# A gated attention kernel in fp32 on one core: the first norm shared out anew, the last products in halves, statistics transposed by VectorE, a sigmoid at the seventh step, a new order of up products and splits

## The chip, the core and the metric

One core of a Trainium2 chip runs the whole kernel. TensorE multiplies, VectorE, ScalarE and GpSimd (POOL) prepare operands and evacuate results, and SyncE (SP) issues most of the DMAs. The metric is the device time of one execution in microseconds; three executions of the kernel before were timed. A profile is one more execution, recorded instruction by instruction.

## The reference

The inputs are `x` (2048 tokens of 640), a key and value cache of 32 heads of which the last 512 positions are used (`W = max(256, 2048 // 4)`), and four weight matrices. Cut to what is computed:

```python
xn = layernorm(x)                                   # over 640, no gain
q = (xn @ wq) split into 32 heads of 128
p = softmax(q k^T * 128 ** -0.5)                    # k, v: the last 512 cached positions
s = (p @ v, heads joined: 4096) @ wo
h = relu(xn @ w1 + b1) ** 2                         # 640 -> 1728
g = silu(h @ w2 + b2)                               # 1728 -> 640
out = x + s * g
```

All of it is float32. The kernel multiplies in TensorE's fp32r form and splits each operand in a high part (a ScalarE copy into fp32r) and a low part (the difference, on VectorE or POOL). A product is then three matmuls, high by high, high by low and low by high (`triple`).

## The kernel before

Tokens are worked in four tiles of 512 (`t` = 0 to 3), columns of `x` in five chunks of 128 (`DC`), the hidden width 1728 in fourteen chunks (`FC`), of which one, `rp` (placed fourth), has 64 columns. The order of the instructions on each engine is the order in which the program text emits them (`Ordered`, line 65); the attention part builds a list of (time, function) pairs, `plan`, and emits it sorted by time.

1. **The first norm** (`ln_first`). Tile 0's four blocks of 128 tokens (`xn[0]` to `xn[3]`) are loaded. VectorE takes mean and variance of each (`bn`, `aggr` into `mv`); blocks 0 and 1 are the first half, 2 and 3 the second. `root(k)` takes the square root of a half's variances on ScalarE and adds eps on VectorE. A reciprocal and a Newton step follow, on POOL for the first half and on VectorE for the second. ScalarE centres and scales blocks 0 and 1 (`centre`, `scale`); VectorE subtracts and multiplies blocks 2 and 3 in one instruction per block and column range (first 256 columns, then 384). TensorE transposes each block chunk by chunk (`turn`) into the five banks `px`; ScalarE copies them out as the high part of `xT` and VectorE takes the low part. The first up product `ph` (`up(0, 0)`, 15 matmuls in an order written out by hand) follows, with the transpose of the bias rows `pb` and what hangs on it (`biases`) behind its sixth matmul.
2. **Tile 0's feed-forward** with the norms of tiles 1 and 2 beside it (`first_step`): per step `f`, an up product of 15 matmuls and the down product of the chunk before, 15 more into the five banks `py`. Weights come in by SP two chunks ahead. The statistics of a later tile lie one token to a partition in `mv` (mean and 1/sd of four blocks: 8 columns). `ln_rows` turns them to rows: a TensorE transpose `pmv`, a copy `lr`, one DMA to DRAM, then two broadcasting loads `mr`. `ln_chunk` uses them two steps later. Tile 3 (`LATE`) gets the same at the last weight pair.
3. **Tiles 1 and 2's up products** in pairs of weight chunks, seven products for eight (`PROD`, `w_first` to `w_third`). VectorE forms sums of the weights (`w_sums`, tile `ws`), ScalarE and VectorE split them (`w_split`, tiles `wa`, `ws`, `wc`, `wl`). The first bank `wa` holds products 1, 6, 7 and 4 in turn; `wy` takes product 5, is copied to `p`, and becomes `wa + p` on VectorE; `wx` likewise after product 7. Between these lie tile 0's gates (`gate`, a sigmoid on ScalarE and a product on VectorE, tile `sg`).
4. **The down products of tiles 1 and 2**, 28 steps `m` of 15 (`c_down`), with operands loaded three steps and split two steps ahead (`c_load`, `c_prep`). After step 13 stands the gate of tile 1, whose five banks the products of tile 2 reuse.
5. **Attention**, 128 units of one head by one tile, a new one each `PERIOD` of 12.4 in the plan. A unit's work: scores `s`, the row maxima by a transposing reduction `rdm`, the shift and exponential `e`, `pt` split on ScalarE and POOL, `o`, and the output product `r`; q products `pq` for two units ahead alternate with these. Into units 0 to 3 goes also the rest of tile 3's up products for the last four chunks (`early_up`, banks `eu`, order in `EARLY_IN`). q products and some of `r` share bank 1.
6. **The end.** Tile 3's feed-forward follows the last unit (`lu`, `ly`). The last four down chunks (`FA` to `FC - 1`) are done column by column (kind `e`, line 1493): 12 matmuls for column `d`, then `late_gate(d)`, a silu, a product with the attention sum `acc`, an addition of `x` and a store. The last column's gate is done in two halves of 256 tokens.

`pe.addr_align` (lines 272, 1317, 1376) puts some TensorE instructions at fixed places of a 256-instruction block.

Of the kernel before, what the change touches and what calls it, by code (L numbers as in the profile page):

```python
# [25 lines left out]
def kernel(  # L26
# [115 lines left out]
    def ln_load(t):  # L142
        mv = xp.tile([P, 4, NB], F32, tag="mv", name=f"mv{t}")[:, :2, :]
        sc = xp.tile([P, 3, NB], F32, tag="sc", name=f"sc{t}")
        xn = []
        for b in range(NB):
            xb = ln_tile(t, b)
            r0 = t * NT + b * P
            nc.sync.dma_start(xb, x[r0 : r0 + P, :])
            xn.append(xb)  # L150
        LS[t] = mv, sc, xn

    def ln_block(t, b):
# [5 lines left out]
        dve.bn_aggr(mv[:, :, b], st)  # L159

# [16 lines left out]
    def ln_rows(t, mv):  # L177
        pm = psx.tile([P, NT], F32, tag="x", name=f"pmv{t}")
        (pe if t == LATE else nc.tensor).transpose(pm[: 2 * NB, :P], mv.rearrange("p a b -> p (a b)"), ident)
        row = xp.tile([2 * NB, P], F32, tag="lr", name=f"lr{t}", bufs=1)  # L180
        nc.vector.tensor_copy(row, pm[: 2 * NB, :P])
        d = dpool.tile([2, NT], F32, name=f"mv_d{t}")
        nc.sync.dma_start(d.rearrange("a (b p) -> (a b) p", p=P), row)
# [65 lines left out]
    def ln_first():  # L249
        mv = xp.tile([P, 4, NB], F32, tag="mv", name="mv0")  # L250
        sc = xp.tile([P, 3, NB], F32, tag="sc", name="sc0")
# [3 lines left out]
        VAR, SD, Y = ([sc[:, i, n * k : n * k + n] for k in range(2)] for i in range(3))  # L255
        warm = mv[:, 3, :1]
        pool.memset(warm, 1.0)
        eps = mv[:, 3, 1:2]
# [45 lines left out]
        def scale(b, cs):  # L304
            js = slice(cs[0] * P, (cs[-1] + 1) * P)
            act.activation(xn[b][:, js], xn[b][:, js], AF.Identity, scale=R[0][:, b : b + 1])

# [14 lines left out]
        centre(1)  # L322
        bn(n, 0)
        dve.reciprocal(Y[0], SD[0])
        newton(0)
        bn(n, 1)
        aggr(n)
        for b in range(n + 1, NB):
            for i in range(2):
                bn(b, i)  # L330
            aggr(b)
        scale(0, range(3))
        root(1)
        scale(0, range(3, DC))
        turn(0, range(DC))
        scale(1, range(DC))
        split_hi(0, raws[0], 0)
        dve.reciprocal(Y[1], SD[1])
        newton(1)
        for cs in (range(2), range(2, DC)):  # L340
            js = slice(cs[0] * P, (cs[-1] + 1) * P)
            for b in range(n, NB):
                m, q = mv[:, 0, b : b + 1], mv[:, 1, b : b + 1]
                dve.tensor_scalar(
                    xn[b][:, js], xn[b][:, js], m, q, op0=ALU.subtract, op1=ALU.mult
                )
            for c in cs:
                for b in range(1, NB):
                    turn(b, (c,))
# [108 lines left out]
    def up(t, f):  # L458
# [15 lines left out]
        for k, (c, i, j) in enumerate(order):  # L474
            pe.matmul(
                ph,
                w[i][:, c, :],
                xs[j][:, c, :],
                start=k == 0,
                stop=k == len(order) - 1,  # L480
            )
            if t == f == 0 and k == 5:
                biases()
# [200 lines left out]

    def w_second(p):
        b = PB[p]
        prod(p, 6, b["a"])
        dve.tensor_tensor(b["y"], b["a"], b["p5"], op=ALU.add)
        prod(p, 2, b["x"])
        rest(p, 0, 0, b["x"])  # L690
        up_end(T1, PAIRS[p][0], b["x"])
# [487 lines left out]
    def late_down(f, ds):  # L1179
# [6 lines left out]
        for d in ds:  # L1186
            dd = slice(d * P, (d + 1) * P)
            if n < P:
                pe.matmul(LPY[d], w[0][:, dd], h[0], start=False, stop=False)
                pe.matmul(LPY[d], w[1][:, dd], h[0], start=False, stop=False)  # L1190
            else:
                triple(
                    LPY[d], (w[0][:, dd], w[1][:, dd]), tuple(h), f == 0, f == FC - 1
                )

# [4 lines left out]

    def late_gate(d):
        py, a = LPY[d], ACC[HALF - 1, TPH - 1][:, d, :]
        sg = ap.tile([P, NT], F32, tag=("bm", "bs")[d % 2], name=f"lsg{d}", bufs=2)
        k = 2 if d == DC - 1 else 1
        js = [slice(i * NT // k, (i + 1) * NT // k) for i in range(k)]
        for j in js:
            act.activation(sg[:, j], py[:, j], AF.Silu, bias=b2_sb[:, d : d + 1])
        for j in js:
            dve.tensor_tensor(a[:, j], sg[:, j], a[:, j], op=ALU.mult)
            dve.tensor_tensor(a[:, j], a[:, j], LR["x"][:, d, j], op=ALU.add)  # L1210
            store(sp, HALF - 1, TPH - 1, d, a, j)

# [16 lines left out]
    w_sums(1)  # L1229
    w_split(1, 0)  # L1230
    w_fifth(0)
    w_second(0)
    gate(0, gate_tile, (3, 4))
    w_split(1, 1)
    w_split(1, 2)
    NP = len(PAIRS)
    for p in range(1, NP):
# [5 lines left out]

        def prepare():
            if more:
                w_split(p + 1, 0)
                w_sums(p + 1)
            else:
                for k in range(2):
                    c_prep(0, k)  # L1250
# [22 lines left out]
    xctx.close()  # L1273
    bctx.close()
    for m in range(2 * FC):
        t, f = CS[m]
        for n in {OPEN + 2: (m + 3, m + 4), OPEN + 3: ()}.get(m, (m + 3,)):
            if n < 2 * FC:
                c_load(n)
# [110 lines left out]
    for i in range(NU):  # L1390
# [65 lines left out]
    for item in order:  # L1456
# [9 lines left out]
        else:  # L1466
            for k, d in enumerate(range(DC)):
                for f in range(FA, FC):
                    DOWN_AT.setdefault(f, now)
                    at(now + 0.68 * ((FC - FA) * k + f - FA), late_down, f, (d,))  # L1470
                at(now + 0.68 * (FC - FA) * (k + 1), late_gate, d)
        now += STEP[kind]
# [110 lines left out]
```

## Time and profile before

| | us |
|---|---|
| median of three runs | 1951.23 (1951.10 to 1951.89) |
| the profiled execution | 1951.11 |
| its span, first to last instruction of the program | 1949.3 |
| TensorE busy | 1941.4, 8576 matmuls |
| VectorE, ScalarE, POOL busy | 1599.3, 1242.6, 1346.5 |
| TensorE's clock as granted | 1.0 |
| HBM traffic | 246.43 MB moved, mean 126 GB/s |

How to read it: a page row of a group has the engine, the operation, what it writes and reads, the shape, the count, busy time, the mean of one in nanoseconds, and the idle time before it with what ended it. A row of the timeline has its start, its length, the engine, the operation and the count of merged instructions, with the idle time before in brackets. A row of the chain of waits has a start, a length and the work that the end hung on then. PEld is the loading of weights, which overlaps the matmuls. A name with q (SPq) is the engine's queue issuing a DMA. Nearly every instruction is recorded in one helper (line 77), so groups are told apart by their tiles.

### The profile page before, as it was taken

Reading aid. Unit: us, or ns where it says so; the run is one execution under the profiler, and the core shown is the slowest. Engines: PE = TensorE matmul, PEld = TensorE weight load, DVE = VectorE, ACT = ScalarE, POOL = GpSimd, SP = SyncE. Lnnn points to the kernel's source line nnn. Section 1 sums busy time; section 2 is a strip of 40 time slices with the busy share of each in tenths; the row PEclk is TensorE's granted clock in tenths of the full one; section 3 lists DMA queues with packets and bytes.
Section 4 is the critical chain, followed back from the end, with each engine's and each line's share of the span. In section 5 each row is a group of like instructions: output and inputs, shape, how many; then the busy total and the mean of one; then the engine's idle time right before and its main releaser. Section 6 shows DMA issues by size and latency. Waiting matters only on the chain.

```text
span 1949.3 us, 28584 instructions
## 1 busy us (share of the span) xinstructions
PE 1941.4 (100%) x8576; PEld 1605.5 (82%) x8576; DVE 1599.3 (82%) x2758; ACT 1242.6 (64%) x2150; POOL 1346.5 (69%) x727
## 2 busy tenths in 40 slices
PE   9999999999999999999999999999999999999998
PEld 7888888888888888888888888888888888888887
DVE  6864747788888888888888878888888888888864
ACT  5665536766666666666666676666666666666643
POOL 0022107888888888888888878888888888888841
PEclk9999999999999999999999999999999999999999
DMA  7557953323233222332335433333333333332353
GB/s 221 184 192 252 366 190 109 95 88 96 90 92 95 91 91 93 92 92 92 93 100 184 140 109 109 114 114 115 114 114 114 114 114 114 97 93 92 85 187 119
DMA packets 147639, 246.43 MB, mean 126 GB/s; under 512 B 25020, under 2 KB 47334, under 8 KB 146214
## 3 DMA queue, kind: packets, MB, share of 16 engines
q1 hardware_dynamic: 144774, 232.64, 38.5%
q0 software_dynamic: 2576, 11.80, 1.5%
q8 instruction: 77, 1.26, 0.2%
q14 instruction: 68, 0.56, 0.1%
q10 hardware_dynamic: 144, 0.16, 0.0%
HBM read 213.59 MB, written 30.95 MB: 125 GB/s over the span
## 4 chain that ended last, share of the span: by engine, by line
PE 99%; DMA 0%; DVE 0%; SPq 0%; issue 0%; ACT 0%
PE pq L77 22%; PE r L77 22%; PE o L77 18%; PE s L77 18%; PE py L77 7%; PE ph L77 3%; PE ly L77 2%; PE wa L77 2%; PE lu L77 2%; PE wy L77 1%; PE wx L77 1%; PE eu L77 1%; DMA xb<-in_x_dram 0%; DMA wr<-in_w_dram 0%; PE px L77 0%; SPq L77 0%
## 5 line engine op out<-in xcount | busy, mean ns | idle before, releaser
L77 POOL TENSOR_TENSOR pt<-e,pt 128x1024 fp32r<-128x1024 f32 x256 | 615.2, 2403 | 113.5 <-ACT pt L77 68.9
L77 PE MATMUL r<-ot,wo 128*128 128x512 f32 x1920 | 496.6, 389 | 0.0
L77 PE MATMUL pq<-ax,wq 128*128 128x512 f32 x1920 | 456.1, 389 | 0.0
L77 PEld LDWEIGHTS pq<-ax,wq 128*128 128x128 f32 x1920 | 360.4, 188 | 75.1 <-DVE q L77 0.4
L77 PEld LDWEIGHTS r<-ot,wo 128*128 128x128 f32 x1920 | 360.5, 188 | 74.8
L77 PE MATMUL o<-pt,wv 128*128 128x512 f32 x1536 | 369.0, 389 | 0.0
L77 PE MATMUL s<-q,wk 128*128 128x512 f32 x1536 | 368.9, 389 | 0.0
L77 DVE TRANSPOSE_TENSOR_REDUCE rdm<-s 128x16 f32<-128x512 f32 x512 | 346.9, 712 | 8.0 <-PE s L77 7.9
L77 ACT ACTIVATE e<-e 128x1024 f32<-128x1024 f32 x256 | 269.7, 1054 | 123.3 <-DVE e L77 83.2
L77 PEld LDWEIGHTS s<-q,wk 128*128 128x128 f32 x1536 | 288.4, 188 | 59.8
L77 PEld LDWEIGHTS o<-pt,wv 128*128 128x128 f32 x1536 | 288.3, 188 | 59.9 <-POOL pt L77 0.2
L77 DVE TENSOR_TENSOR e<-s,bm 128x512 f32<-128x512 f32 x512 | 312.3, 665 | 5.3 <-DMA bm<-m_d 4.3
L77 POOL TENSOR_TENSOR su<-e,e 128x1024 f32<-128x1024 f32 x128 | 308.8, 2412 | 0.0
L77 ACT ACTIVATE pt<-e 128x1024 fp32r<-128x1024 f32 x256 | 272.0, 1062 | 6.9
L77 DVE TENSOR_TENSOR acc<-r,acc 128x512 f32<-128x512 f32 x300 | 203.6, 679 | 12.7 <-PE r L77 12.4
L77 ACT ACTIVATE rdm<-rdm 32x64 f32<-32x64 f32 x384 | 97.7, 255 | 182.3 <-DVE rdm L77 179.2
L77 DVE TENSOR_TENSOR ot<-o,ot 128x512 fp32r<-128x512 f32 x128 | 88.6, 692 | 86.1 <-ACT ot L77 86.1
L77 DVE TRANSPOSE_TENSOR_REDUCE rds<-su 128x32 f32<-128x1024 f32 x128 | 158.3, 1237 | 0.3 <-POOL su L77 0.3
L77 ACT ACTIVATE q<-pq 128x512 fp32r<-128x512 f32 x128 | 76.8, 600 | 120.0 <-PE pq L77 120.0
L77 ACT ACTIVATE rds<-rds 32x32 f32<-32x32 f32 x384 | 89.7, 234 | 60.0 <-DVE rds L77 56.6
L77 POOL TENSOR_TENSOR wo<-or,wo 128x640 fp32r<-128x640 f32 x64 | 101.0, 1578 | 30.1 <-ACT wo L77 30.1
L77 POOL TENSOR_TENSOR wv<-vr,wv 128x512 fp32r<-128x512 f32 x64 | 83.2, 1300 | 53.6 <-ACT wv L77 53.6
(171 smaller groups left out, 2005.3 us busy)
## 6 DMA issues: line engine op xcount, KB each, us to landing
bm<-m_d SPq DMA_DIRECT2D x128, 256.0 KB, 3.2
bs<-s_d SPq DMA_DIRECT2D x128, 256.0 KB, 4.0
qr<-in_wq_dram SPq DMA_DIRECT2D x64, 320.0 KB, 4.7
or<-in_wo_dram SPq DMA_DIRECT2D x64, 320.0 KB, 4.6
kr<-in_kT_dram SPq DMA_DIRECT2D x64, 256.0 KB, 4.4
vr<-in_v_dram SPq DMA_DIRECT2D x64, 256.0 KB, 4.4
cw<-in_w_dram SPq DMA_DIRECT2D x26, 320.0 KB, 4.5
h_m<-r SPq DMA_DIRECT2D x26, 256.0 KB, 2.1
```

The source lines that it names most:

```text
L77: ins = method(*args, **kwargs)
```

## The change

- **Norm of tile 0.** The first half's reciprocal and Newton step are emitted ahead of block 2's statistics. ScalarE scales block 0 in one piece, then centres the first 256 columns of block 2 (with minus its mean, `less`, made by POOL) and later scales them. POOL scales block 1. Block 1's transposes follow block 0's. VectorE keeps block 3 and the rest of block 2.
- **Biases.** `biases()` is emitted behind the first matmul of the first product, not the sixth.
- **`ln_rows`.** `mv` has 32 columns (those behind the first 8 cleared by POOL in `ln_load`); VectorE transposes it in blocks of 32 and four DMAs write the four groups of rows to DRAM.
- **Weight splits.** `w_split(1, 0)` moves into `w_second(0)`, behind the sum into `wy`; `w_split(1, 1)` and `w_split(1, 2)` move into `prepare` of pair 1, behind the sum into `wx`.
- **Sigmoid.** At step `m == 6` a sigmoid of one column is emitted on ScalarE.
- **Up products.** All four `early_up` groups of unit 1 come ahead of its q product (planned at 5.6 rather than 4.2, its low part 6.4 behind that rather than 4.1).
- **Last products.** The last column's 12 matmuls become 24 of 256 tokens: first all of the first half, its gate and store, then the second half. Its second half is moved to a bank of its own ahead of that, by a ScalarE copy (`late_seed`).

```diff
     def ln_load(t):
-        mv = xp.tile([P, 4, NB], F32, tag="mv", name=f"mv{t}")[:, :2, :]
+        mv = xp.tile([P, 32 // NB, NB], F32, tag="mv", name=f"mv{t}")
+        nc.gpsimd.memset(mv[:, 2:, :], 0.0)
...
     def ln_rows(t, mv):
-        pm = psx.tile([P, NT], F32, tag="x", name=f"pmv{t}")
-        (pe if t == LATE else nc.tensor).transpose(pm[: 2 * NB, :P], mv.rearrange("p a b -> p (a b)"), ident)
-        row = xp.tile([2 * NB, P], F32, tag="lr", name=f"lr{t}", bufs=1)
-        nc.vector.tensor_copy(row, pm[: 2 * NB, :P])
+        row = xp.tile([P, B32], F32, tag="lr", name=f"lr{t}", bufs=1)
+        nc.vector.transpose(row, mv.rearrange("p a b -> p (a b)"))
         d = dpool.tile([2, NT], F32, name=f"mv_d{t}")
-        nc.sync.dma_start(d.rearrange("a (b p) -> (a b) p", p=P), row)
+        to = d.rearrange("a (b p) -> (a b) p", p=P)
+        for g in range(0, P, B32):
+            nc.sync.dma_start(to[:, g : g + B32], row[g : g + 2 * NB, :])
...
         centre(1)
-        bn(n, 0)
         dve.reciprocal(Y[0], SD[0])
         newton(0)
-        bn(n, 1)
+        for i in range(2):
+            bn(n, i)
         aggr(n)
+        pool.tensor_scalar(less, mv[:, 0, n : n + 1], -1.0, 0.0, op0=ALU.mult, op1=ALU.add)
...
-        scale(0, range(3))
+        scale(0, range(DC))
+        act.activation(xn[n][:, : 2 * P], xn[n][:, : 2 * P], AF.Identity, bias=less)
+        pool.tensor_scalar(xn[1], xn[1], mv[:, 1, 1:2], None, op0=ALU.mult)
         root(1)
-        scale(0, range(3, DC))
         turn(0, range(DC))
-        scale(1, range(DC))
         split_hi(0, raws[0], 0)
+        turn(1, range(DC))
         dve.reciprocal(Y[1], SD[1])
         newton(1)
         for cs in (range(2), range(2, DC)):
             js = slice(cs[0] * P, (cs[-1] + 1) * P)
-            for b in range(n, NB):
+            if cs[0] == 0:
+                scale(n, cs)
+            for b in range(n + 1 if cs[0] == 0 else n, NB):
...
-                for b in range(1, NB):
+                for b in range(n, NB):
                     turn(b, (c,))
...
-            if t == f == 0 and k == 5:
+            if t == f == 0 and k == 0:
                 biases()
...
-    def w_second(p):
+    def w_second(p, between=None):
         b = PB[p]
         prod(p, 6, b["a"])
         dve.tensor_tensor(b["y"], b["a"], b["p5"], op=ALU.add)
+        if between:
+            between()
         prod(p, 2, b["x"])
...
+    def late_half(f, j):
+        w, h = LW[2, f], LH[f]
+        dd, js = slice((DC - 1) * P, DC * P), slice(j * NT // 2, (j + 1) * NT // 2)
+        triple(
+            LPY[DC - 1, j],
+            (w[0][:, dd], w[1][:, dd]),
+            [v[:, js] for v in h],
+            False,
+            f == FC - 1,
+            skip_group_check=True,
+        )
+
+    def late_seed():
+        py, m = LPY[DC - 1], NT // 2
+        LPY[DC - 1, 0] = py[:, :m]
+        LPY[DC - 1, 1] = bank("ly5", FA % 2)[:, :m]
+        act.activation(LPY[DC - 1, 1], py[:, m:], AF.Copy)
...
-    w_split(1, 0)
     w_fifth(0)
-    w_second(0)
+    w_second(0, lambda: w_split(1, 0))
     gate(0, gate_tile, (3, 4))
-    w_split(1, 1)
-    w_split(1, 2)
...
         def prepare():
+            if p == 1:
+                w_split(1, 1)
+                w_split(1, 2)
             if more:
                 w_split(p + 1, 0)
                 w_sums(p + 1)
...
+        if m == 6:
+            act.activation(table, b2_sb[:, :1], AF.Sigmoid)
...
-            qs = [(i + 2, 4.9 if i == 3 else 4.2, 4.1)]
+            qs = [(i + 2, {1: 5.6, 3: 4.9}.get(i, 4.2), 6.4 if i == 1 else 4.1)]
...
+            at(now, late_seed)
+            for d in range(DC):
+                k = 2 if d == DC - 1 else 1
+                for j in range(k):
+                    for f in range(FA, FC):
+                        DOWN_AT.setdefault(f, now)
+                        if k == 1:
+                            at(now, late_down, f, (d,))
+                        else:
+                            at(now, late_half, f, j)
+                        now += 0.68 / k
+                    py = (d, j) if k > 1 else d
+                    at(now, late_gate, d, py, j * NT // k, (j + 1) * NT // k)
...
-            first = EARLY_IN[n - 2] < u or u == 3
+            first = EARLY_IN[n - 2] < u or u in (1, 3)
```

More of the change, by code (lines that the diff above doesn't have):

```diff
@@ L158, in ln_block @@
             dve.bn_stats(st[:, i, :], xn[b][:, i * hd : (i + 1) * hd])
-        dve.bn_aggr(mv[:, :, b], st)
+        dve.bn_aggr(mv[:, :2, b], st)
     def ln_var(t):
@@ L249, in ln_first @@
     def ln_first():
-        mv = xp.tile([P, 4, NB], F32, tag="mv", name="mv0")
+        mv = xp.tile([P, 32 // NB, NB], F32, tag="mv", name="mv0")
         sc = xp.tile([P, 3, NB], F32, tag="sc", name="sc0")
@@ L256, in ln_first @@
         warm = mv[:, 3, :1]
+        less = mv[:, 2, :1]
         pool.memset(warm, 1.0)
@@ L305, in scale @@
             js = slice(cs[0] * P, (cs[-1] + 1) * P)
-            act.activation(xn[b][:, js], xn[b][:, js], AF.Identity, scale=R[0][:, b : b + 1])
+            act.activation(
+                xn[b][:, js], xn[b][:, js], AF.Identity, scale=mv[:, 1, b : b + 1]
+            )
         def turn(b, cs):
@@ L1191, in late_down @@
             else:
-                triple(
-                    LPY[d], (w[0][:, dd], w[1][:, dd]), tuple(h), f == 0, f == FC - 1
-                )
+                last = FA if d == DC - 1 else FC
+                triple(LPY[d], (w[0][:, dd], w[1][:, dd]), tuple(h), f == 0, f == last - 1)
+    def late_half(f, j):
[8 more added lines that the diff above has]
+            skip_group_check=True,
+        )
+    def late_seed():
[3 more added lines that the diff above has]
+        act.activation(LPY[DC - 1, 1], py[:, m:], AF.Copy)
     def late_x():
@@ L1199, in late_x, with late_gate @@
             sp.dma_start(LR["x"][:, d, :], xT[d * P : (d + 1) * P, LATE * NT : (LATE + 1) * NT])
[L1201 to L1211, printed above, removed]
+    def late_gate(d, py, lo, hi):
+        a, j = ACC[HALF - 1, TPH - 1][:, d, :], slice(lo, hi)
+        tag = ("bm", "bs")[(d + lo * 2 // NT) % 2]
+        sg = ap.tile([P, NT], F32, tag=tag, name=f"lsg{d}_{lo}", bufs=2)[:, : hi - lo]
+        act.activation(sg, LPY[py], AF.Silu, bias=b2_sb[:, d : d + 1])
+        dve.tensor_tensor(a[:, j], sg, a[:, j], op=ALU.mult)
+        dve.tensor_tensor(a[:, j], a[:, j], LR["x"][:, d, j], op=ALU.add)
+        store(sp, HALF - 1, TPH - 1, d, a, j)
     for f in range(FC):
@@ L1274 @@
     bctx.close()
+    table = cpool.tile([P, 1], F32, name="table")
     for m in range(2 * FC):
         t, f = CS[m]
+        if m == 6:
+            act.activation(table, b2_sb[:, :1], AF.Sigmoid)
         for n in {OPEN + 2: (m + 3, m + 4), OPEN + 3: ()}.get(m, (m + 3,)):
@@ L1466 @@
         else:
[L1467 to L1471, printed above, removed]
+            at(now, late_seed)
[11 more added lines that the diff above has]
+                    at(now, late_gate, d, py, j * NT // k, (j + 1) * NT // k)
         now += STEP[kind]
```

## The prediction

> All times are microseconds from the start of the profiled span unless a sentence says otherwise.
>
> **What bounds the kernel now.** I read the page's busy table and the shares of its chain first, then the waits of the weight loads, which show every place where TensorE lacked something.
>
> ```profile
> span 1949.3 us, 28584 instructions
> PE 1941.4 (100%) x8576; PEld 1605.5 (82%) x8576; DVE 1599.3 (82%) x2758; ACT 1242.6 (64%) x2150; POOL 1346.5 (69%) x727
> ...
> PE 99%; DMA 0%; DVE 0%; SPq 0%; issue 0%; ACT 0%
> ```
>
> ```profile
> PEld py L77 <- DVE sg L77: 0.5, 1, 0.5
> PEld pq L77 <- DVE q L77: 0.4, 1, 0.4
> PEld wa L77 <- DVE wx L77: 0.2, 1, 0.2
> PEld wa L77 <- DVE wa L77: 0.2, 1, 0.2
> ```
>
> TensorE is the chain. After the first norm it waits at four places in all, for about half a microsecond or less. So the middle of the kernel can only give back those waits and the TensorE work that is removed; a larger sum has to come from the first twelve microseconds or from what follows the last product. What a stop costs is read from the chain of waits, where a run of products that never stops takes 3.40 for 15, which is 0.2267 each.
>
> ```profile
> 22.28 3.40 PE ph L77 x15
> ...
> 40.48 0.11 PE pmv L179
> ...
> 177.49 0.11 PE pmv L77
> ...
> 119.50 2.82 PE wa L77 x12
> ...
> 125.72 2.13 PE wa L77 x9
> ...
> 237.04 8.04 PE py L77 x34
> ...
> 306.99 3.70 PE pq L77 x15
> ```
>
> Twelve products should take 2.72, nine 2.04, 34 7.71 and fifteen 3.40. So the stops cost 0.10, 0.09, 0.33 and 0.30. The two rows of pmv are the first and last of three transposes of statistics, 0.11 of TensorE each.
>
> **The change, part by part.** The sum is made against the profiled execution: its span is 1949.3, its own time 1951.11, so 1.8 lies around the span and stays. The median of the three runs, 1951.23, is 0.12 above that time.
>
> *Statistics transposed by VectorE.* Three transposes leave TensorE: 3 x 0.11 = **-0.33**. VectorE does one transpose of 128x32 in place of its copy out of the bank; the nearest row is the 32x32 transpose, 0.20, and VectorE is not what TensorE waits for there. SP issues four small DMAs for one, 0.30 each, three times: some 0.9 more on SP ahead of the broadcasts mr and of later loads. That is hidden: the rows are used two steps of 6.8 (an up and a down of 3.40) later. Without that cover it would be 0.9 in each of three places. The three clears of mv on POOL fall where POOL idles or copies for stores.
>
> ```profile
> L77 DVE STREAM_TRANSPOSE rows<-sq 32x32 f32<-32x32 f32 x128 | 25.6, 200 | 4.5 <-DVE sq L77 0.2
> 40.94 0.30 SPq L183 DMA_DIRECT2D mv_d<-lr  x1
> ```
>
> *The sigmoid at the seventh step.* It pulls the table load out of the place where the second tile's products wait for the gate of the first.
>
> ```profile
> 207.37 0.63 ACT L77 ACTIVATE xT<-xc 128x512 fp32r<-128x512 f32 x1 [2.47 <-DVE xc L77]
> ...
> 234.22 1.28 ACT L77 ACT_TABLE_LOAD   x1
> ...
> 235.51 3.00 ACT L77 ACTIVATE sg<-py,b_sb 128x512 f32<-128x512 f32 x5
> 236.24 3.39 DVE L77 SCALAR_TENSOR_TENSOR sg<-py,b_sb,sg 128x512 f32<-128x512 f32 x5 [1.18 <-ACT sg L77]
> ```
>
> VectorE's first gate product then ends about 1.2 sooner, near 235.8, and TensorE wants that bank at 236.8: the whole stop goes, **-0.33**. At the seventh step the load and a one-column activation cost ScalarE some 1.5, against idle time of 2.47 there (the row at 207), with operands prepared two steps ahead: nothing. Without that cover up to 1.5.
>
> *The order of the early up products.* In attention unit 1 the fourth q product now follows all four early up groups (two more, 1.36), while VectorE finishes splitting the previous q. That split ends at 306.93 and the product would start 1.36 after 306.96. **-0.30**. Its own two split halves move behind the next unit's weight splits and the four shifts on VectorE. That pushes the next row maxima by at most one split, 0.65, whose bank is not wanted for a further unit: nothing, or up to 0.65 if that cover is gone.
>
> ```profile
> 306.28 0.65 DVE L77 SCALAR_TENSOR_TENSOR q<-pq,q 128x512 fp32r<-128x512 f32 x1
> ```
>
> *The order of the weight splits.* This is the one edit that I price as a loss. The second pair's first split now comes behind the sum into wy on VectorE.
>
> ```profile
> 117.61 1.18 POOL L77 TENSOR_TENSOR r<-r 64x512 f32<-64x512 f32 x1 [0.60 <-ACT r L77]
> 117.82 1.26 DVE L77 TENSOR_TENSOR ws<-wp,ws 128x256 f32<-128x256 f32 x1
> ...
> 119.00 0.68 DVE L77 TENSOR_TENSOR wa<-wp,wa 128x512 fp32r<-128x512 f32 x1
> 119.61 0.69 DVE L77 TENSOR_TENSOR wy<-wa,p 128x512 f32<-128x512 f32 x1
> ...
> 119.74 0.75 PEld L77 LDWEIGHTS wa<-xT,wa 128*128 128x128 f32 x4 [0.21 <-DVE wa L77]
> ```
>
> VectorE is occupied until 119.0 by the four weight sums. Now wa ends at 119.68, and the weight load that waits for it starts at 119.74. With wy first, at 119.0, wa starts at about 119.61 and ends at 120.3, so that load, the third of its product, comes 0.61 later with nothing else for TensorE to do: **+0.61**. Behind it the stop at 125.7 goes (0.09), since two further splits no longer stand ahead of the sum into wx, and a little of the 0.10 at 119.5: **-0.10** together. The two moved splits have until the fifth product of pair 1, nine products (2.04) after the seventh product's end; sum and first split take 0.70 and 0.68 of that. Bounds of this part: -0.19 if VectorE comes earlier than these rows say, +0.61 + 0.68 if ScalarE's half also is late.
>
> *The share of the first norm.*
>
> ```profile
> 5.84 0.29 ACT L77 ACTIVATE sc<-mv 128x2 f32<-128x2 f32 x1 [0.22 <-DVE mv L77]
> 6.45 0.15 DVE L77 RECIPROCAL sc<-sc 128x2 f32<-128x2 f32 x1
> 7.51 0.20 POOL L77 TENSOR_TENSOR mv<-mv,sc 128x2 f32<-128x2 f32 x1
> 8.26 0.29 ACT L77 ACTIVATE sc<-mv 128x2 f32<-128x2 f32 x1
> 8.46 1.21 ACT L77 ACTIVATE xb<-xb,mv 128x256 f32<-128x256 f32 x2
> 9.38 1.51 DVE L77 TENSOR_SCALAR xb<-xb,mv 128x256 f32<-128x256 f32 x4
> 10.53 2.56 ACT L77 ACTIVATE xT<-px 128x512 fp32r<-128x512 f32 x5 [0.24 <-PE px L77]
> 11.09 1.58 POOL L77 TENSOR_TENSOR w1s<-w1r,w1s 128x640 fp32r<-128x640 f32 x1
> 11.33 0.60 PE L77 MATMUL px<-ident,xb 128*128 128x128 f32 x4
> ...
> 13.32 0.11 PE pb L77
> ...
> 1943.95 0.84 ACT L77 ACTIVATE lsg<-ly,b_sb 128x256 f32<-128x256 f32 x2 [2.03 <-PE ly L77]
> ```
>
> The first reciprocal moves ahead of a statistics instruction, from 6.45 to just behind the first root (6.13), 0.27 sooner. POOL's Newton step then ends at 7.44 (7.71 before) and ScalarE scales block 0 from 7.47. Behind it ScalarE centres 256 columns of block 2; a pair of these two widths took 1.21 at 8.46 and its follower started some 0.1 before its end, so the second root starts at 8.59 in place of 8.26: 0.33 late. From root to the first normalised columns it was 1.12 (8.26 to 9.38), so block 2 is scaled from 9.71 on ScalarE, ready at 10.18 (0.47 for 256 columns, read from the pair of gate activations at 1943.95, which takes 0.84 with an overlap), and block 3 beside it on VectorE. Two transposes with their drain take 0.5, and the first copy xT starts near 10.70 against 10.53: 0.17 late. The first group's fifth product needs the second of these copies. Against that the bias transpose pb goes from behind the sixth product into a pause behind the first, -0.11. Together **+0.07**. POOL's new scaling of block 1 (no such row; single-source work there is nearest to the 640-wide subtraction, 1.58, from above and to the two-column row, 0.20, from below) starts at 7.7 and ends by 9.3, ahead of need, since block 1's transposes come ahead of 10.2. Bounds: -0.11 and the rival below.
>
> *The last products as halves.* The last column of products is done in two halves of 256, with the first half's gate, product and store under the second half.
>
> ```profile
> 1944.92 0.42 DVE L77 TENSOR_TENSOR acc<-acc,lx 128x256 f32<-128x256 f32 x1
> ...
> 1945.71 0.42 DVE L77 TENSOR_TENSOR acc<-acc,lx 128x256 f32<-128x256 f32 x1
> ...
> L77 PEld LDWEIGHTS ly<-lh,l2w 128*128 128x128 f32 x205 | 38.5, 188 | 8.0
> ```
>
> Behind the last product stands one half in place of two: the end of VectorE's work moves from 1946.13 to 1945.34, **-0.79**, and the last store with it. Twelve full products (2.72) become 24 halves. Before has no half product. From below it is half of 0.2267, 0.113; from above a full one, if the weight load of 0.188 sets the pace. I take 0.12, as loads start with the product before and lie beneath it: 24 x 0.12 - 2.72 = **+0.16** (bounds 0.00 and +2.72). The copy that seeds the second bank lies under ten microseconds of other columns' products.
>
> [...]
>
> **Sum:** -0.33 - 0.33 - 0.30 + 0.61 - 0.10 + 0.07 - 0.79 + 0.16 = **-1.01**, so 1950.1 for a profiled execution and **1950.2** for the median.
>
> **The rivals.** *The reorderings cost nothing*: the wa split is not late and the head gains its 0.11. For it speaks that both orders hold the same VectorE work; against it that VectorE is the last releaser at 119.74. Without 0.61 and with -0.11 for +0.07 the time is 1949.4.
>
> *The weight load paces the halves* (the slower side). Place: the last 24 products. The 0.188 of a load and the 0.039 idle between loads make 0.227, the very pitch of a full product, so a half could cost a full slot: +2.72 instead of +0.16, time 1952.8. From 0.162 per half on (2.72 plus the 1.17 that the rest saves, over 24) the kernel is slower than before. Against it: 128-wide transposes, with loads of the same number of columns, ran four in 0.60 at 11.33, a pitch of 0.11.
>
> *POOL holds up VectorE in the head.* At 117.82 a VectorE subtraction of 256 columns, for which other such rows have 0.42, took 1.26, until POOL's square was over. If POOL's scaling of block 1 lasts until 9.3 and holds VectorE's small sums of the second half so long, its reciprocal starts at 9.3 in place of 8.9 (the second root's end, 8.59 + 0.29) and all that follows is 0.4 later: 1950.6. [...]
>
> *The two waits come back elsewhere*: the change does not do what it says for the table load and the q product, 0.33 and 0.30 stay, 1950.8. Against it: both have slack of a microsecond in the rows above.
>
> **How the numbers follow.** Forecast 0.41, reorderings free 0.20, halves paced by loads 0.12, POOL in the head 0.12, waits back 0.07, and 0.08 for something that no row shows, such as the places that the hand alignment of TensorE's code gives to fewer instructions. The forecast's own range is 1949.6 to 1950.8. The range of 8 in 10 starts at the lowest sum of the bounds (0.19 and 0.11 won, halves at 0.00: 2.05 off) less the spread of runs, 1948.9, and ends at the weight-load rival, 1952.9. About 0.2%, 3.9 us, is what a measurement can tell from no change. No case but the unseen 0.08 gets there, and mostly on the slower side: all stops and the whole tail do not add up to 3.9. Faster 0.02, within 0.92, slower 0.06.
>
> **What would show it.** No pmv on TensorE; no stop behind sg near 237 and behind q near 307; 34 products there in 7.71. A stop of about 0.65 behind wa near 119.5 if the loss is real, none if the first rival is. The half products' pitch in the last 2.9. The first xT copy at 10.7 (10.5 or earlier: the head gained; 11.1: POOL held it). One half behind the last product, ending 0.79 sooner against it. The forecast is wrong if TensorE's chain shows a stop that before did not have.

## The result and the profile after

| | before | after |
|---|---|---|
| median of 5 runs, us | 1951.46 (1951.1 to 1952.33) | 1983.73 (1983.5 to 1984.02) |
| ratio | | 1.0165, 95% interval 1.0153 to 1.0176 |
| span of the profiled execution, us | 1949.3 | 1981.9 |
| granted clock of TensorE | 1.0 | 1.0 |

The kernel became 32 us slower; the prediction was 1950.2. First the page of the changed kernel (busy time of TensorE and of its weight loads; then the shares of the chain that ended last), then the waits of its weight loads.

```profile
PE 1973.9 (100%) x8585; PEld 1605.4 (81%) x8585; DVE 1615.5 (82%) x2757; ACT 1245.6 (63%) x2152; POOL 1350.3 (68%) x732
...
PE 98%; DVE 1%; ACT 0%; DMA 0%; POOL 0%; issue 0%; SPq 0%; DVEq 0%; POOLq 0%
```

```profile
PEld px L77 <- ACT xb L77: 1.3, 1, 1.3
PEld px L77 <- POOL xb L77: 1.0, 1, 1.0
PEld wa L77 <- DVE wa L77: 0.5, 1, 0.5
```

TensorE is still the whole chain, and behind the first norm it waits for something only once, for half a microsecond. The waits behind sg and q are gone as predicted. So the 32 us are not idle time: TensorE is busy for 1973.9 in place of 1941.4, with nine matmuls more. The groups of its instructions show where (busy time of a group in us, then the mean length of one in ns, in which successive products overlap), before and after:

```profile
L77 PE MATMUL r<-ot,wo 128*128 128x512 f32 x1920 | 496.6, 389 | 0.0
L77 PE MATMUL pq<-ax,wq 128*128 128x512 f32 x1920 | 456.1, 389 | 0.0
L77 PE MATMUL o<-pt,wv 128*128 128x512 f32 x1536 | 369.0, 389 | 0.0
L77 PE MATMUL s<-q,wk 128*128 128x512 f32 x1536 | 368.9, 389 | 0.0
L77 PE MATMUL py<-ch,cw 128*128 128x512 f32 x410 | 93.6, 389 | 0.0
```

```profile
L77 PE MATMUL r<-ot,wo 128*128 128x512 f32 x1920 | 509.6, 396 | 0.0
L77 PE MATMUL pq<-ax,wq 128*128 128x512 f32 x1920 | 459.1, 390 | 0.0
L77 PE MATMUL o<-pt,wv 128*128 128x512 f32 x1536 | 379.0, 395 | 0.0
L77 PE MATMUL s<-q,wk 128*128 128x512 f32 x1536 | 373.7, 392 | 0.0
L77 PE MATMUL py<-ch,cw 128*128 128x512 f32 x410 | 93.3, 389 | 0.0
```

Every matmul has the same shape as before, and the counts are the same, yet r costs 13.0 more, o 10.0, s 4.8 and pq 3.0, while py costs nothing more: 30.8 in four groups of the attention, a part of the kernel that the change hardly touches. The timeline of TensorE in the attention shows it group by group (start, length, name, number); a length includes the drain, the 0.16 in which the last product runs out while the next group has begun. Before, then after:

```profile
603.65 2.88 PE L77 MATMUL o<-pt,wv 128*128 128x512 f32 x12
606.37 1.52 PE L77 MATMUL r<-ot,wo 128*128 128x512 f32 x6
607.73 2.88 PE L77 MATMUL s<-q,wk 128*128 128x512 f32 x12
610.45 1.52 PE L77 MATMUL r<-ot,wo 128*128 128x512 f32 x6
```

```profile
610.90 2.96 PE L77 MATMUL o<-pt,wv 128*128 128x512 f32 x12
613.70 1.56 PE L77 MATMUL r<-ot,wo 128*128 128x512 f32 x6
615.10 2.92 PE L77 MATMUL s<-q,wk 128*128 128x512 f32 x12
617.86 1.56 PE L77 MATMUL r<-ot,wo 128*128 128x512 f32 x6
```

From one start to the next, twelve o took 2.72 before and take 2.80, 233 ns in place of 227 for one; six r take 1.40 for 1.36; twelve s 2.76 for 2.72. The pitch, the time from the start of one product to the start of the next, has changed in a stream that never waits.

What the change did to these products is their place in memory. A tile has an address within a partition of SBUF; in the built programs, those of the left side are stacked behind the constants, those of the right side (ax, wq, wk, q, wv, wo, and T and xT of tile 1 before them) come down from the top. The new constant `table` has four bytes and takes 32. All left tiles behind it move up by 32 bytes: `ot` from 38400 to 38432, `pt` from 84480 to 84512. `wo` stays at 123904, `wv` at 220672. Before, every tile of these products started on a multiple of 512. In r and o the streamed tile (ot, pt) now starts 32 bytes off its weights (wo, wv); in py<-ch,cw, where both are left tiles that moved together, the pitch has stayed.

### The profile page after: what moved, and what is told of

The parts are those of the page before. It is cut to its first block, busy times and chain, and to the rows that moved or that the text cites. A ratio compares the mean times of both kernels' runs of the same rounds, so it can differ in the third digit from the quotient of the medians.

```text
span 1981.9 us, 28629 instructions
## 1 busy us (share of the span) xinstructions
PE 1973.9 (100%) x8585; PEld 1605.4 (81%) x8585; DVE 1615.5 (82%) x2757; ACT 1245.6 (63%) x2152; POOL 1350.3 (68%) x732
## 3 DMA queue, kind: packets, MB, share of 16 engines
q8 instruction: 77, 1.26, 0.2%
## 4 chain that ended last, share of the span: by engine, by line
PE 98%; DVE 1%; ACT 0%; DMA 0%; POOL 0%; issue 0%; SPq 0%; DVEq 0%; POOLq 0%
PE r L77 23%; PE pq L77 22%; PE o L77 18%; PE s L77 18%; PE py L77 7%; PE ly L77 2%; PE ph L77 2%; PE wa L77 2%; PE lu L77 2%; PE wy L77 1%; PE wx L77 1%; PE eu L77 1%; DVE T L77 0%; ACT r L77 0%; DMA xb<-in_x_dram 0%; DVE ws L77 0%
## 5 line engine op out<-in xcount | busy, mean ns | idle before, releaser
L77 PE MATMUL r<-ot,wo 128*128 128x512 f32 x1920 | 509.6, 396 | 0.0
L77 PE MATMUL o<-pt,wv 128*128 128x512 f32 x1536 | 379.0, 395 | 0.0
L77 PE MATMUL s<-q,wk 128*128 128x512 f32 x1536 | 373.7, 392 | 0.0
L77 DVE TRANSPOSE_TENSOR_REDUCE rdm<-s 128x16 f32<-128x512 f32 x512 | 353.6, 716 | 10.5 <-PE s L77 10.1
```

Source lines behind the costliest of these rows:

```text
L77: ins = method(*args, **kwargs)
```

## The experiments

"Distance" below is the start of the left side's tiles (pt, ot) less that of the right side's (wv, wo, wq, wk, q, ax), modulo 256.

| kernel | distance | us | its kernel before | ratio, 95% interval |
|---|---|---|---|---|
| the change | 32 | 1983.73 | 1951.46 | 1.0165 (1.0153 to 1.0176) |
| change, tile of 64 bytes | 64 | 1977.01 | 1952.09 | 1.0129 (1.0113 to 1.0144) |
| before, with a tile of 4 bytes | 32 | 1984.77 | 1952.09 | 1.0169 (1.0154 to 1.0184) |
| change, both sides moved | 64 | 1976.99 | 1952.09 | 1.0128 (1.0113 to 1.0143) |
| before, right side moved down 32 | 32 | 1985.04 | 1952.09 | 1.0170 (1.0153 to 1.0187) |
| change, spare column | 0 | 1950.36 | 1951.84 | 0.9993 (0.9984 to 1.0002) |
| before, tile of 128 bytes | 128 | 1979.58 | 1951.84 | 1.0142 (1.0128 to 1.0157) |
| before, tile of 256 bytes | 0 | 1951.86 | 1951.84 | 0.9999 (0.9990 to 1.0009) |
| change, all on 512 | 0 | 1950.48 | 1951.84 | 0.9993 (0.9984 to 1.0002) |
| the same, one split put back | 0 | 1949.80 | 1952.18 | 0.9988 (0.9979 to 0.9997) |
| before, pt alone moved 32 | 32 in o | 1967.01 | 1952.18 | 1.0077 (1.0063 to 1.0091) |
| before, q and wk moved 32 | 0 in s | 1961.10 | 1951.85 | 1.0049 (1.0032 to 1.0066) |
| before, tile of 192 bytes | 192 | 1981.57 | 1951.85 | 1.0153 (1.0138 to 1.0168) |

**1. The tile alone, and two rival rules.** Four kernels were to tell an effect of places from one of TensorE's code or order.

```diff
-    table = cpool.tile([P, 1], F32, name="table")
+    table = cpool.tile([P, 16], F32, name="table")
...
-            act.activation(table, b2_sb[:, :1], AF.Sigmoid)
+            act.activation(table[:, :1], b2_sb[:, :1], AF.Sigmoid)
```

> The changed kernel, with its new tile of one column made sixteen columns (64 bytes instead of 4; the activation still writes one column). No instruction changes, only the addresses behind the tile: in the changed kernel the tiles of the left side start 32 bytes past a multiple of 64 and those of the right side on one, here all start on a multiple of 64, as before the change. Theory A (a product is slower where its moving tile and its weight tile start at different places within 64 bytes): all groups of products back to 226.7 ns, and 1949 to 1952 us, the changed kernel's 1983.7 less some 8,600 products x 3.8 ns = 33. Theory B (a tile that doesn't start on a multiple of 64 bytes is read more slowly, wherever the other one lies): the same here, it is told apart by the third run. Theory C (the order or the code of TensorE's instructions, as the change left them, sets the pitch): no change, 1983 to 1985.

On the kernel before, the tile alone, with no instruction that uses it:

```diff
     bctx.close()
+    table = cpool.tile([P, 1], F32, name="table")
     for m in range(2 * FC):
```

> The kernel before, with only a tile of one column (4 bytes) added where the change adds one; nothing writes or reads it, so that no instruction is added, taken or moved. The left side's tiles move by 32 bytes, the right side's stay. Theories A and B: the groups r<-ot,wo, o<-pt,wv and the wa, wx, wy groups at about 233 ns as in the changed kernel, py<-h,w2s and py<-ch,cw at 226.7 by A, slower too by B; time 1951.4 + 33 = 1982 to 1986. Theory C: 1951.4, as before.

On the changed kernel, and then on the kernel before, the right-hand pools moved too:

```diff
-                    pad(xr, 480)
+                    pad(xr, 512)
...
-    at(10.0, pad, pools["ep"], 480)
+    at(10.0, pad, pools["ep"], 512)
```

> The changed kernel with its tile of 4 bytes, and the filler of the two right-hand pools 512 instead of 480 bytes, so that their tiles start 32 bytes past a multiple of 64 as well: no tile of a product starts on a multiple of 64, and all agree. No instruction changes. Theory A: every group at 226.7 ns, 1949 to 1952. Theory B: every group slow, 8,500 products x 6.7 ns = 57 above the kernel before, about 2007, in no case below the changed kernel's 1983.7. Theory C: 1983 to 1985.

> The kernel before with the filler of the two right-hand pools 512 instead of 480 bytes: the right side's tiles (ax, wq, wk, q, wv, wo, T, xT of tile 1, l1w, l2w) start 32 bytes past a multiple of 64, the left side's (ot, pt, ws, wa, wl, h, w2s, ch, cw) on one. Theory A: the same pairs disagree as in the changed kernel, so r, o and the wa group at about 233 ns, s and pq at 228 to 230, 1982 to 1986. Theory B: r, o, s and pq slow at 233 ns each, 6,900 products x 6.7 = 46, so about 1997. Theory C: 1951.4.

The second settles the main question: with an unused tile of four bytes and not one instruction changed, the kernel before takes 1984.77. Theory C is out as the cause. TensorE's row for 600 to 1000 us (the length of the window, the busy time, the number of matmuls, the granted clock, DMA share and rate) in the kernel before, in this kernel, and in the first one:

```profile
600.00:1000.00 400.00, 400.00 (x1766) 1.00 0.30 91
```

```profile
600.00:1000.00 400.00, 400.00 (x1731) 1.00 0.29 90
```

```profile
600.00:1000.00 400.00, 400.00 (x1739) 1.00 0.30 91
```

400 us divided by these counts is 226.5, 231.1 and 230.0 ns. The clock is 1.00 in all three, and the DMA load is the same.

But the first and the third missed every expectation: 1977 both times, where A said 1950, B said 1950 and 2007, and C 1984. Theory B is out with them, since moving both sides made the changed kernel faster, not slower. What they share is the distance. In the third the right side's tiles, moved down by 32, start at 480 within 512, so the left side's, at 32, are 64 ahead modulo 256, as in the first. Two kernels with different places and the same distance have the same time to 0.02 us. So the distance counts, but "within 64 bytes" was wrong: the modulus is larger. The fourth fits as well: left tiles at 0, right ones at 480, the distance is 32 modulo 256 again, and the time that of the second.

**2. How far apart is far enough.**

```diff
-    table = cpool.tile([P, 1], F32, name="table")
...
-            act.activation(table, b2_sb[:, :1], AF.Sigmoid)
+            act.activation(b_sb[:, 95:], b2_sb[:, :1], AF.Sigmoid)
```

> The changed kernel without its new tile: the sigmoid writes a spare column of the tile of biases. From the attention on every tile of a product starts on a multiple of 512 bytes again, as before the change. Between 60 and 315 us the tiles behind the smaller row tile stay 256 bytes off that grid (their tile of statistics is larger, the row tile smaller), the right side's not. Theory A2 (what counts is the distance between the two tiles' starts, modulo some number over 64, since distances of 32 and of 64 bytes both cost): r, o, s and pq at 226.7 ns; 1950 to 1951.5 if that number divides 256, and some 2.5 us more (about 400 products of 100 to 200 us at 6 ns) if it is 512. Theory C (the changed order or code of TensorE's instructions has a cost of its own, some 25 us, which the first run kept): 1975 to 1978, with r, o, s, pq at 229 to 231 ns.

On the kernel before, the unused tile with 32 columns, then with 64:

> The kernel before with an unused tile of 32 columns (128 bytes) where the change adds its tile: left and right side 128 bytes apart. Theory A2: 1951 to 1952.5 and 226.7 ns everywhere if the number is 128; in the changed kernel the weight tiles of py<-ch,cw lie 0 and 128 bytes from their moving tiles, and that group kept 226.7 ns, which speaks for it. If the number is 256 or 512: 1970 to 1985. Theory C: 1951 to 1952.5.

> The same with a tile of 64 columns (256 bytes). Theory A2: 1951 to 1952.5 if the number is 128 or 256, 1970 to 1985 if it is 512. Theory C: 1951 to 1952.5.

And the kernel with the spare column, with the row tile enlarged so that the tiles of the second stage are back on multiples of 512 too:

```diff
-        row = xp.tile([P, B32], F32, tag="lr", name=f"lr{t}", bufs=1)
+        row = xp.tile([P, 3 * B32], F32, tag="lr", name=f"lr{t}", bufs=1)[:, :B32]
```

> The changed kernel with the sigmoid in the spare column and the row tile 384 bytes instead of 128, so that all tiles of products between tile 1's first step and the end start on multiples of 512 again: what the rest of the change does by itself. Theory A2: the prediction's sum without its missed term, 1 us below the kernel before, ratio 0.9990 to 1.0000; every group at 226.7 ns. Theory C: 1975 to 1978.

128 bytes cost 27.7 us, 256 cost nothing (1951.86 against 1951.84): at the distances tried, the modulus is 256. The hint from py<-ch,cw was wrong: the tiles cw at 128 bytes are the raw weights as loaded; the split ones that TensorE reads lie with ch. The tiles 256 bytes off the grid in the spare-column kernel cost nothing either (1950.36, against 1950.48 with all on 512). Without the distance the rest of the change is within the measurement, 1.4 us faster than before by the medians, with an interval that includes no change. Not quite every tile is back in the kernel with all on 512: the change's larger statistics tile stands ahead of the up weights of the 64-column chunk and keeps them 128 bytes off their streams. That is three groups of ten products in the whole kernel. In the changed kernel, where two of the three are 128 bytes off as well, they take 2.32 to 2.33 each from start to start (the first from 29.26 to 31.59) where before had 2.30, less than 0.1 us together.

**3. Which products meet.** The kernel before, with pt alone moved:

```diff
     def p_hi(i, k):
+        first = not PT
+        if first:
+            ap.tile([P, 8], F32, name="pad0", bufs=1)
         PT[i, k] = [
...
         ]
+        if first:
+            ap.tile([P, 120], F32, name="pad1", bufs=1)
```

> The kernel before with 32 bytes of filler ahead of the tiles pt alone and 480 behind them, so that all others stay on multiples of 512. Theory A3 (what counts is the distance of the two tiles of a product, modulo 256, and it acts in the products of that pair and in some behind them until the pitch has settled): o<-pt,wv at 233 ns, 1,536 x 6.7 = 10 us; r<-ot,wo directly behind o slow in its first 6, as s and pq are in the changed kernel behind r, 128 x 6 x 4.5 ns = 3.5 us, and a few products of the groups behind these; the rest at 226.7: 1963 to 1968. If a distance acts in its own pair alone: 1961 to 1962.5, r at 226.7 throughout. If tiles off the common grid slow all products: 1980 or more.

```profile
607.52 2.97 PE L77 MATMUL o<-pt,wv 128*128 128x512 f32 x12
610.33 1.55 PE L77 MATMUL r<-ot,wo 128*128 128x512 f32 x6
611.72 2.89 PE L77 MATMUL s<-q,wk 128*128 128x512 f32 x12
614.45 1.52 PE L77 MATMUL r<-ot,wo 128*128 128x512 f32 x6
```

Twelve o take 2.81, the six r behind them 1.39 although ot and wo agree, s 2.73 from start to start. The time, 14.8 over the kernel before, lies in the range of A3. So a disagreement slows its own products and six or seven behind them.

Then q and wk were moved together. They are the two tiles of the products s, so s agrees with itself and differs from its neighbours.

```diff
     def prep(kind, hf, h, eng=None):
...
+        if kind == "k" and not KT:
+            pools["ep"].tile([P, 8], F32, name="pad0", bufs=1)
...
     def q_hi(i):
+        first = not Q
         Q[i] = pair("q", [P, NT], f"q{i}", AHEAD + 1)
+        if first:
+            pools["ep"].tile([P, 56], F32, name="pad1", bufs=1)
...
-    at(10.0, pad, pools["ep"], 480)
+    at(10.0, pad, pools["ep"], 224)
```

> The kernel before with q and wk, the two tiles of the products s, both moved by 32 bytes, and all other tiles kept on multiples of 256 (filler of 32 bytes ahead of wk and 224 behind q; the copies of the last tile's h that live in the same places move too). Within s the distance is 0; between a product of s and its neighbours of other groups it is 32: while the last product ahead of s streams, the first weights wk are loaded, and while the last of s streams, the next group's weights are. If the distance acts between a product's own two tiles alone: s, r and pq at 226.7 ns, 1951.5 to 1952.6 (some products ly slower). If it acts between a stream and the weights that are loaded under it, and upsets the products behind for as long as in the changed kernel (some 30 ns in 8 products): twice 128 such meetings, 7 to 9 us, 1959 to 1962, with the first products of s and those directly behind s slow.

```profile
605.25 2.88 PE L77 MATMUL o<-pt,wv 128*128 128x512 f32 x12
607.97 1.53 PE L77 MATMUL r<-ot,wo 128*128 128x512 f32 x6
609.34 2.92 PE L77 MATMUL s<-q,wk 128*128 128x512 f32 x12
612.10 1.55 PE L77 MATMUL r<-ot,wo 128*128 128x512 f32 x6
613.48 3.56 PE L77 MATMUL pq<-ax,wq 128*128 128x512 f32 x15
```

o keeps 2.72; the r ahead of s takes 1.37, s 2.76, the r behind it 1.38: slow are the last product ahead of s, the first of s and the first behind s, though each of them agrees with its own weights. Product by product, between 600 and 1000 us, the last r ahead of s takes 235 ns and so does the last s; the product before each of them takes 227. 9.25 us over the kernel before is the second theory's number, not the first's. A distance therefore acts between a tile that streams and the weights that are loaded under it for the next product (in the kernel before the load of the first weights of o begins at 603.42, when the last r ahead of it starts, and o at 603.65). Within a group these are the group's own two tiles, which is why the groups of the changed kernel could be sorted by them. It also accounts for s and pq there, which lost 4.8 and 3.0 though their own tiles agree: both follow r, whose last stream disagrees with their first weights, and only the first eight s and the first five pq differ from 227 ns (231 on the mean between 600 and 1000 us).

**4. The size by distance.**

> The kernel before with an unused tile of 48 columns (192 bytes) where the change adds its tile. Theory A3 (distance modulo 256): 192 is 64 the other way round. If the sign doesn't matter, as 32 one way and the other gave the same 33 us, the time is that of a distance of 64, 1976 to 1979. If the price is by the lowest set bit of the address (64 in both), it is the same number; if only by how far the two are apart without wrapping, it is another, 1970 to 1990.

1981.57 is 29.7 over the kernel before; a distance of 64 cost the changed kernel 26.6 over its own time at 0 (1977.01 against 1950.36). The expectation of 1976 to 1979 missed. It also rested on a wrong premise: the fourth kernel's distance is not the second's reversed, it is the same, as said above. So no run had tried the sign before this one, and 64 and 192 differ. The price is 33 us at 32, 27 at 64, 28 at 128, 30 at 192, and no rule for it came out.

**5. The loss that the prediction did price.** On the kernel with all tiles on 512:

```diff
+    w_split(1, 0)
     w_fifth(0)
-    w_second(0, lambda: w_split(1, 0))
+    w_second(0)
```

> The previous kernel (all tiles on multiples of 512), with the split of the next pair's first weights ahead of the sum wy again, as before the change; the two later splits stay where the change put them. In the previous kernel's trace TensorE stops for 0.63 us behind the wa product that begins at 119.67 us. If that stop is VectorE's order alone, as the prediction's sum has it, some 0.06 us of it is left (286 ns instead of 227, as in the kernel before) and the time is 0.57 us shorter: 1949.9, ratio about 0.9990, a difference at the edge of what the time can tell, so that the trace decides. The rival: the stop moves to the places behind it (125.6 and 177.4, as before the change) and 0.2 to 0.6 us of it stays.

TensorE's timeline without this edit, then with it:

```profile
119.44 0.61 PE L77 MATMUL wa<-xT,wa 128*128 128x512 f32 x2
120.42 1.20 PE L77 MATMUL wa<-xT,wa 128*128 128x512 f32 x4 [0.36 <-DVE wa L77]
121.45 1.53 PE L77 MATMUL wa<-T,ws 128*128 128x512 f32 x6
```

```profile
119.81 1.72 PE L77 MATMUL wa<-xT,wa 128*128 128x512 f32 x6
121.37 1.53 PE L77 MATMUL wa<-T,ws 128*128 128x512 f32 x6
```

Six products from start to start: without the edit 2.01 (119.44 to 121.45), with it 1.56, against 1.36 without any stop. So 0.45 of a stop of 0.65 went and 0.20 stayed; 0.06 was expected. The time, 1949.8, is what was expected, but it differs from that of the kernel without the edit (1950.48) by less than the intervals' width, and this execution has another short wait (0.3, of py for r, near 193 us) that the other had not. It is the one kernel of the study whose interval lies below 1: ratio 0.9988 (0.9979 to 0.9997).

## Why the prediction was wrong

**The step that failed** stands under *The sigmoid at the seventh step*: "At the seventh step the load and a one-column activation cost ScalarE some 1.5, against idle time of 2.47 there (the row at 207), with operands prepared two steps ahead: nothing." The activation was priced as time on ScalarE alone. Its result needs a tile, the tile takes 32 bytes ahead of every left-side tile, and those 32 bytes cost 33 us (the second run: the tile without the activation). The code showed the place: a new constant allocated ahead of pools whose fillers of 480 bytes keep the other side on a grid.

**The last sentence of the forecast failed too**: "The forecast is wrong if TensorE's chain shows a stop that before did not have." It was wrong without any stop that accounts for it. I took 0.2267 per product as a property of the shape and looked only for waits. **The unseen case** had 0.08 and named the alignment of TensorE's code; the runs showed the alignment of data, with the code untouched.

**The rest of the sum**, read from the kernel with all tiles on 512, whose span is 1948.8 against 1949.3, so -0.5 where the sum had -1.01:

| term | predicted | shown |
|---|---|---|
| three transposes pmv | -0.33 | gone, none on TensorE |
| stop behind sg | -0.33 | gone |
| stop behind q | -0.30 | gone |
| wa split behind wy | +0.61 | +0.55 |
| stops behind it | -0.10 | -0.09 |
| head | +0.07 | +0.34 |
| one half behind the last product | -0.79 | -0.80 |
| halves | +0.16 | +0.16 |
| a wait in the attention (this execution) | none | +0.33 |
| sum | -1.01 | -0.47 |

TensorE's timeline of this kernel shows the two stops gone: 63 products py in 14.44 (14.28, and 0.16 of drain), and pq beginning 2.72 after the twelve early up products did.

```profile
227.76 14.44 PE L77 MATMUL py<-ch,cw 128*128 128x512 f32 x63
...
305.51 2.88 PE L77 MATMUL eu<-xT,w1s 128*128 128x512 f32 x12
308.23 3.56 PE L77 MATMUL pq<-ax,wq 128*128 128x512 f32 x15
```

*The wa split* is close: 2.01 less 1.36 is a stop of 0.65 (the rows of the fifth experiment), where before had one of 0.10. So is *the tail*:

```profile
1940.13 4.17 PE L77 MATMUL ly<-lh,l2w 128*128 128x512 f32 x29
...
1945.30 0.42 DVE L77 TENSOR_TENSOR acc<-acc,lx 128x256 f32<-128x256 f32 x1
```

The matmuls end at 1944.30 and VectorE at 1945.72, 1.42 later; before it was 1946.13 less 1943.91 (the end of the last row of ly below), 2.22. The difference is 0.80. The row of 29 holds five full products and 24 halves; less a drain of 0.16 (2.88 less 2.72 in a group of twelve) it is 4.01, and less 5 x 0.227 it leaves 2.88, 0.120 for a half. The weight load did not pace the halves.

```profile
1940.80 3.11 PE L77 MATMUL ly<-lh,l2w 128*128 128x512 f32 x13
```

*The head* was mis-sized. The first product py before, then rows of the head in the kernel with all tiles on 512:

```profile
18.72 3.56 PE L77 MATMUL py<-h,w2s 128*128 128x512 f32 x15
```

```profile
7.61 1.89 POOL L77 TENSOR_SCALAR xb<-xb,mv 128x640 f32<-128x640 f32 x1
...
8.88 0.17 DVE L77 RECIPROCAL sc<-sc 128x2 f32<-128x2 f32 x1 [0.33 <-ACT sc L77]
...
9.27 0.16 DVE L77 TENSOR_TENSOR mv<-mv,sc 128x2 f32<-128x2 f32 x1
9.35 0.74 ACT L77 ACTIVATE w1s<-w1r 128x640 fp32r<-128x640 f32 x1 [0.51 <-DMA w1r<-in_w_dram]
...
10.00 0.49 ACT L77 ACTIVATE xb<-xb,mv 128x256 f32<-128x256 f32 x1
11.02 2.56 ACT L77 ACTIVATE xT<-px 128x512 fp32r<-128x512 f32 x5 [0.53 <-PE px L77]
19.06 3.56 PE L77 MATMUL py<-h,w2s 128*128 128x512 f32 x15
```

The first py begins at 19.06 in place of 18.72. The reciprocal came at 8.88, where the sum had it (8.59 + 0.29). What I left out is the split of the first weights, `split_hi`, which stands ahead of block 2's scaling on ScalarE: it waits for a DMA until 9.35, and the scaling begins at 10.00, not 9.71. The first copy xT is at 11.02, not 10.70. *The rival of POOL in the head* is out, although its sign, a first copy at 11.1, was nearly there: POOL scaled block 1 from 7.61 to 9.50 (1.89, where the prediction's nearest row from above had 1.58), and the reciprocal and the small sums on VectorE ran beneath it at 0.16 to 0.17 each. The sum at 9.27 has two inputs, as has the subtraction at 117.82 before, which the prediction read as held (1.26 in place of 0.42). What sets the two apart was not tried.

*The wait in the attention* was not in the sum. In this execution one product o waits for POOL's split of pt:

```profile
1082.60 1.00 PEld L77 LDWEIGHTS o<-pt,wv 128*128 128x128 f32 x5 [0.48 <-POOL pt L77]
```

The wait costs 0.33 with what follows it on TensorE (443 and 338 ns from start to start for two products, less 2 x 227, 0.33). The prediction read four waits behind the first norm; the same list has a fifth, of a weight load of o for pt, and the kernel before with the unused 256-byte tile, which runs the same instructions, shows two that are longer. These two rows, in that order:

```profile
PEld o L77 <- POOL pt L77: 0.2, 1, 0.2
```

```profile
PEld o L77 <- POOL pt L77: 0.7, 2, 0.4
```

The changed kernel and the one with the split put back have none of 0.15 or more. So this wait comes and goes without the change's instructions, and no run shows it to be a cost of the change; without it the rows add up to -0.80. What sets it off was not tried.

The sizes of the change's own parts were thus right to about 0.3 us, and the forecast of 1950.2 lies close to the time of the changed kernel without its four-byte tile, 1950.36. That closeness is partly luck: the head was 0.27 off, and the kernel before, measured beside that run, took 1951.84 where the forecast started from 1951.23. The cause of the 32 us is shown by runs. How TensorE comes to lose time by the distance is not: that the two reads meet in the memory is my guess from which products are slow, and no trace shows it.

## What to carry to other kernels

A new tile, however small, moves all that is allocated behind it (four bytes moved it by 32 here); where streams and weights lie on different sides or in different pools, keep both on one grid (256 bytes here), or write small results into a spare column. When TensorE is busy throughout and the kernel still got slower, compare the distance between starts in groups that the change didn't touch before looking for waits. And test an address effect with an unused tile: it changes nothing else.

## What the hardware showed that was not expected

- The pitch of 128x512 fp32r matmuls depended on where the streamed tile starts against the weights being loaded for the next product, modulo 256 bytes: 227 ns at 0 (2.72 for twelve), 233 ns at 32 (2.80). With engines, instructions and granted clock unchanged, a shift of the left side's tiles by 32 bytes costs 1.69% of the kernel (1.54 to 1.84%, the kernel before with an unused tile of 4 bytes).
- The loss outlasts its cause. Behind a group that disagrees, the next products stay slow though they agree: six r took 1.39 in place of 1.36 with pt alone moved, and two such meetings per s group cost 9.25 us over the kernel with q and wk moved.
- Which end of 256 bytes the distance lies at matters little, but it matters: 64 cost 27 us and 192 cost 30.
